# Batch 0's token softmax and reads in mid-run, with its x loaded a second time, and a new order of all steps

## The chip, the cores and the metric

One core of one Trainium2 chip. The metric is device time in microseconds (us) of one launch. The kernel before takes 210.89 us, the median of three runs (210.84 to 211.17).

## The reference

Eight batches, each of eight heads with 512 tokens and 32 states of 64 numbers, attend in both directions; the results go, 4352 rows of 512, through a two-layer network with a Prelu of its own slope for each of 2048 hidden columns.

```python
scores = scale * np.matmul(x, state.transpose(0, 1, 3, 2))
a = softmax(scores)                                  # over the 32 states
xread = np.matmul(a, state)                          # 512 rows a batch
scores2 = scale * np.matmul(state, x.transpose(0, 1, 3, 2))
a2 = softmax(scores2)                                # over the 512 tokens
sread = np.matmul(a2, x)                             # 32 rows a batch
rows = concatenate([xread, sread])                   # heads side by side
h = rows @ w_in
out = (maximum(h, 0) + alpha * minimum(h, 0)) @ w_out
```

## The kernel before, in words

Everything is one function. Every piece of work is a named step, and a table of tokens, `ORDER`, says in which order the steps are given to the engines: `F.1.9.4` is "first product of batch 1, hidden block 9, in PSUM bank k4", and the letter `a`, `v` or `p` at some tokens picks ScalarE (ACT), VectorE (DVE) or GpSimd (POOL). Each engine works its part of the list strictly in that order and waits where an operand is not there yet. DMAs that cast (x, states, w_in, w_out) are issued from POOL, transposing DMAs and the stores of the output from SyncE (SP).

For a batch b below 8 the rows of attention never exist as such. Steps `m` and `mo` form state times w_in for a quarter f of the hidden columns (`m_b_f`, L521, casts L545 and L547). The state softmax turns scores into weights: `sc` (L314), `sb` (a transpose in 32x32 blocks, L346), `smax` (L379), `ssh` (subtract the maximum, L384, on POOL), `sexp` (L393), `ssum` (L400, L401), `snorm` (L404), `wb` (transposed back, L412). Then `F` multiplies weights and m into h (L570), `N` takes the negative part of h on ACT (L623), and `G` makes the Prelu g on DVE (L626). Batch 0 is treated differently while the kernel starts: its state softmax runs in two halves on scores that have the tokens in the partitions (`tsc`, `at`), and four of its 16 hidden blocks are made by half parts `f`, `n`, `g` (L592, L607, L611).

The second layer is plain for batch 0 (`S`, L640, eight pairs for each of four blocks of 128 rows, and `O` for its output). For the other batches a scheme with seven in place of eight products is used: POOL or DVE form sums of g (`U`, L707) and of w_out (`W`, L683), `P` are the products (L728, four matmuls of 256 columns each), `K` and `Q` put the output together (L744, L759, L761).

The token softmax is the other direction: `tm` (maximum over 512 tokens, L424), `nb` (times -scale), `te` (exponential with its sum, L441), `tsum` (reciprocal), `tn` (each exponential times the reciprocal, L457 on ACT or L459 on POOL), `tt` (a transposing DMA), `rd` (times x, L475) and `rdo` (out of PSUM into `reads`, L486). After four batches `rt` and `rto` turn the reads into columns XS, and the 256 rows of all state reads make up a ninth batch: its `F` (L579) contract XS with w_in.

x is loaded by `lx` into one of three buffers xg (L161); `xd` transposes it by DMA. For batches 0 and 1 `xt` and `xo` do so by matmuls and copies (L299, L304), and batch 0's x comes without a cast through SP in two halves that `cx` casts (L177). The states of batch 0 come in a small early load through ACT, all others in one load `lst` through POOL. `Z` are fills: matmuls of a pattern that nobody reads.

Of the kernel before, what the change touches and what calls it, by code (L numbers as in the profile page):

```python
# [8 lines left out]
F32 = mybir.dt.float32  # L9
# [13 lines left out]
m.1.0 mo.1.0.v f.0.0.0.2 n.0.1.0 snorm.p.0.1 xt.1.0.0.0 at.1.1 ao.1.v n.0.0.0 xo.1.0.1.a g.0.1.0.0 g.0.0.0.1 m.0.1.3.1
xo.1.0.0.a sc.1 m.2.0.4.0 mo.0.1.a.1 mo.0.1.a.0 mo.2.0.a.0 g.0.0.0.0 S.0.2.0.1 mo.2.0.a.1 tm.1 sb.1 F.0.5.2 F.0.4.3
nb.1.a wo.1 g.0.1.0.1 wi.3 f.0.1.1.4 N.0.5 G.0.5 F.0.6.0 te.1.0 smax.1 N.0.4 S.0.2.1 G.0.4 F.0.7.5 te.1.1 f.0.0.1.2
m.0.2 N.0.6 n.0.1.1 G.0.6 g.0.1.1.1 mo.0.2.a g.0.1.1.0 wo.2 wo.3 tsum.0 S.0.1.2.3 S.0.2.2 F.0.11.0 N.0.7 G.0.7 ssh.p.1
n.0.0.1 F.0.10.4 g.0.0.1.0 g.0.0.1.1 S.0.1.1 N.0.11 G.0.11 sexp.1 ssum.1.5 m.0.3 mo.0.3.a S.0.2.3 S.0.1.3 S.0.1.0
m.1.1 N.0.10 G.0.10 tn.0.0.p mo.1.1.a tn.0.1.p tt.0 F.0.9.2 snorm.v.1 F.0.8.0 N.0.8 m.1.3 N.0.9 G.0.9 S.0.1.5 mo.1.3.a
W.1.0.p F.0.14.4 N.0.14 F.0.15.5 N.0.15 S.0.2.5 m.1.2 mo.1.2.a G.0.8 S.0.2.4 wb.1 lx.2 G.0.14 xd.2 F.0.13.2 N.0.13
S.0.1.4 F.1.5.0 N.1.5 F.0.12.4 G.0.15 S.0.1.7 W.2.0.p F.1.1.5 G.0.13 W.3.0.p S.0.2.7 N.0.12 G.0.12 tsum.1 F.1.6.2  # L30
W.3.1.p G.1.5 N.1.1 W.1.1.p G.1.1 N.1.6 G.1.6 S.0.1.6 F.1.4.4 F.1.12.0 O.0.1.a N.1.4 N.1.12 G.1.4 F.1.8.5 N.1.8 G.1.12
F.1.15.3 F.1.2.2 G.1.8 S.0.2.6 N.1.15 G.1.15 W.2.1.p S.0.0.3.4 N.1.2 S.0.0.1 rd.0.0 lx.3 tn.1.0.a sc.2 O.0.2.a G.1.2
m.2.2.5.3 mo.2.2.a.1 rdo.0.a sb.2 tn.1.1.p mo.2.2.a.0 F.1.3.1 tm.2 S.0.3.0.2 W.4.1.p F.1.0.3 N.1.0 smax.2 N.1.3 G.1.3
S.0.3.4 F.1.13.0 N.1.13 S.0.0.5 nb.2.a te.2.1 S.0.3.2 ssh.p.2 G.1.0 U.1.3.0.p F.1.7.5 N.1.7 te.2.0 G.1.7 tsum.2
S.0.3.6 S.0.3.5 S.0.3.7 F.1.14.1 N.1.14 G.1.13 S.0.3.3 G.1.14 tn.2.0.p tt.1 U.1.1.1.p U.1.2.1.p xd.3 sexp.2 S.0.0.2
m.2.3.3.5 m.4.3 mo.2.3.a.0 ssum.2.0 mo.2.3.a.1 S.0.0.0 F.1.9.1 N.1.9 mo.4.3.a G.1.9 S.0.3.1 S.0.0.6 O.0.3.a snorm.v.2
P.1.2.0.1.3 F.1.11.5 N.1.11 G.1.11 wb.2 m.3.2 mo.3.2.a S.0.0.7 F.1.10.1 N.1.10 G.1.10 S.0.0.4 O.0.0.a rd.1.2 rdo.1.a
m.3.0.0.5 mo.3.0.a.1 lx.4 xd.4 sc.3 tm.3 P.1.2.1.1 mo.3.0.a.0 sb.3 F.2.9.4 N.2.9 G.2.9 nb.3.a F.2.11.2 F.2.10.5
# [63 lines left out]
def kernel(  # L102
# [710 lines left out]
```

## Time and profile before

| | |
|---|---|
| median of three runs | 210.89 us |
| the profiled execution | 210.96 us, of which its span is 209.2 us |
| PE busy | 199.0 us (95%) |
| DVE busy | 182.0 us (87%) |
| POOL busy | 165.6 us (79%) |
| ACT busy | 150.9 us (72%) |
| read from HBM / written | 17.31 / 8.91 MB |

Times in the profile run from the start of the span. A group's row gives line, engine, operation, out<-in with shapes, count, then busy us and mean ns of one, then the idle time just before and what ended it. A matmul's own duration overlaps the next one's: what a matmul costs in a row of many is the step from start to start. The same holds in a smaller measure for DVE and ACT.

### The profile page before, as it was taken

Reading aid. Unit: us, or ns where it says so; the run is one execution under the profiler, and the core shown is the slowest. Engines: PE = TensorE matmul, PEld = TensorE weight load, DVE = VectorE, ACT = ScalarE, POOL = GpSimd, SP = SyncE. Lnnn points to the kernel's source line nnn. Section 1 sums busy time; section 2 is a strip of 40 time slices with the busy share of each in tenths; the row PEclk is TensorE's granted clock in tenths of the full one; section 3 lists DMA queues with packets and bytes.
Section 4 is the critical chain, followed back from the end, with each engine's and each line's share of the span. In section 5 each row is a group of like instructions: output and inputs, shape, how many; then the busy total and the mean of one; then the engine's idle time right before and its main releaser. Section 6 shows DMA issues by size and latency. Waiting matters only on the chain.

```text
span 209.2 us, 5108 instructions
## 1 busy us (share of the span) xinstructions
PE 199.0 (95%) x2024; PEld 132.9 (64%) x2024; DVE 182.0 (87%) x275; ACT 150.9 (72%) x293; POOL 165.6 (79%) x105
## 2 busy tenths in 40 slices
PE   7787799999999999999999999999999999999993
PEld 2453333443667677666577776667778777788882
DVE  0899999999999999999999999999899868595750
ACT  3799998999999889998897748956876386423000
POOL 8244599899999999998999999897981999504640
PEclk9999999999999999999999999999999999999999
DMA  6999999698586698269981572034201111013142
GB/s 167 219 204 206 206 188 130 154 156 161 120 104 147 125 93 194 68 90 168 141 109 39 104 165 97 12 93 127 75 3 53 50 50 53 0 50 103 60 150 95
DMA packets 49992, 23.71 MB, mean 113 GB/s; under 512 B 34480, under 2 KB 49456, under 8 KB 49968
## 3 DMA queue, kind: packets, MB, share of 16 engines
q0 software_dynamic: 17792, 8.09, 30.1%
q1 hardware_dynamic: 31904, 15.22, 29.6%
q8 instruction: 16, 0.26, 0.5%
q10 hardware_dynamic: 272, 0.07, 0.1%
q14 instruction: 8, 0.07, 0.1%
HBM read 17.31 MB, written 8.91 MB: 125 GB/s over the span
## 4 chain that ended last, share of the span: by engine, by line
PE 61%; DMA 12%; DVE 11%; POOL 11%; issue 1%; ACT 0%; SPq 0%; POOLq 0%; DVEq 0%
PE px L728 19%; PE h L570 16%; PE pv L728 9%; POOL gsum L707 7%; DVE g L626 6%; PE py L728 6%; DMA w_in_sb<-in_moe_w_in_dram 5%; DMA st<-in_state_dram 4%; PE h L579 3%; PE o L640 2%; PE m_ps L521 2%; DMA xT<-xg 2%; DMA e2T<-e 2%; DVE oq L761 1%; DVE nb L424 1%
## 5 line engine op out<-in xcount | busy, mean ns | idle before, releaser
L626 DVE SCALAR_TENSOR_TENSOR g<-neg,oma_sb,h 128x512 f16<-128x512 f32 (+1 forms) x140 | 92.3, 707 | 7.4 <-ACT neg L623 6.8
L623 ACT ACTIVATE neg<-h 128x512 f32<-128x512 f32 (+1 forms) x140 | 75.1, 579 | 20.6 <-PE h L570 15.5
L570 PE MATMUL h<-aT,m 128*128 128x512 f16 x248 | 67.3, 379 | 0.2
L728 PEld LDWEIGHTS <-gsum 128*128 128x128 f16 x480 | 46.2, 98 | 13.0 <-issue 1.5
L728 PEld LDWEIGHTS <-g 128*128 128x128 f16 x360 | 35.1, 98 | 11.2 <-issue 0.9
L707 POOL TENSOR_TENSOR gsum<-g,g 128x1024 f16<-128x1024 f16 (+1 forms) x14 | 27.8, 1990 | 11.6 <-DVE g L626 7.2
L707 POOL TENSOR_TENSOR gsum<-gsum,g 128x1024 f16<-128x1024 f16 (+1 forms) x15 | 30.0, 2003 | 8.3 <-DVE gsum L707 7.5
L570 PEld LDWEIGHTS <-m 128*128 128x128 f16 x248 | 23.8, 98 | 16.1 <-issue 1.9
L728 PE MATMUL px<-ws,gsum 128*128 128x256 f16 x240 | 32.8, 273 | 0.0
L707 POOL TENSOR_TENSOR gsum<-g 128x1024 f16<-128x1024 f16 (+1 forms) x14 | 28.8, 2064 | 0.8 <-PE pv L728 0.8
L707 POOL TENSOR_TENSOR gsum<-g,gsum 128x1024 f16<-128x1024 f16 x12 | 25.4, 2130 | 0.2
L744 ACT COPY kept<-px 128x512 f32<-128x512 f32 (+1 forms) x20 | 11.5, 577 | 11.3 <-PE px L728 9.5
L547 ACT CAST m<-m_ps 128x512 f16<-128x512 f32 x33 | 18.0, 604 | 1.9 <-PE m_ps L521 1.7
L640 PE MATMUL o<-w_out_sb,g 128*128 128x512 f16 x64 | 17.5, 380 | 1.8 <-DVE g L626 1.0
L384 POOL TENSOR_TENSOR ts<-ts,mx 128x1024 f32<-128x1024 f32 x7 | 13.4, 1913 | 5.9 <-DVE mx L379 5.9
L728 PE MATMUL py<-w_out_sb,g 128*128 128x256 f16 x120 | 17.5, 273 | 0.1
L728 PE MATMUL px<-w_out_sb,g 128*128 128x256 f16 x120 | 16.7, 272 | 0.1
L728 PE MATMUL px<-w_out_sb,gsum 128*128 128x256 f16 x120 | 16.7, 273 | 0.0
L728 PE MATMUL pv<-ws,gsum 128*128 128x256 f16 x120 | 16.1, 273 | 0.0
L728 PE MATMUL pv<-ws,g 128*128 128x256 f16 x120 | 15.7, 273 | 0.0
L761 DVE TENSOR_TENSOR oq<-pv,kept 128x512 f32<-128x512 f32 (+1 forms) x16 | 10.4, 652 | 5.2 <-PE pv L728 4.8
L521 PE MATMUL m_ps<-w_in_sb,stT 64*32 64x512 f16 x256 | 12.6, 384 | 1.1 <-DMA w_in_sb<-in_moe_w_in_dram 0.4
(84 smaller groups left out, 253.6 us busy)
## 6 DMA issues: line engine op xcount, KB each, us to landing
out_dram<-oq SPq DMA_DIRECT2D x28, 256.0 KB, 2.7
xg<-in_x_dram POOLq DMA_DIRECT2D x7, 512.0 KB, 7.1
w_in_sb<-in_moe_w_in_dram POOLq DMA_DIRECT2D x4, 512.0 KB, 11.3
w_out_sb<-in_moe_w_out_dram POOLq DMA_DIRECT2D x4, 512.0 KB, 13.4
x<-in_x_dram SPq DMA_DIRECT2D x2, 512.0 KB, 5.0
out_dram<-osb SPq DMA_DIRECT2D x4, 256.0 KB, 2.7
out_dram<-oq SPq DMA_DIRECT2D x4, 128.0 KB, 2.1
st<-in_state_dram POOLq DMA_DIRECT2D x1, 224.0 KB, 7.5
```

The source lines that it names most:

```text
L384: engine(e).tensor_tensor(blocks(cols(live["ts", b], j, S)), blocks(scored(b, j)), over_blocks(cols(live["mx", b], j, S // N)), ALU.subtract,)
L521: nc.tensor.matmul(t[N * k : N * (k + 1), :], st_head(b, h)[64 * r : 64 * r + 64, :], w_in_sb[64 * r : 64 * r + 64, c, 512 * f : 512 * (f ...
L547: copier(e)(m_tile(b, f)[:, g, :], t[g])
L570: nc.tensor.matmul(h.rearrange("p (r j s) -> p r j s", r=2, j=2), ms[b, f][:, g, 128 * j : 128 * (j + 1)], weights(b, g), start=(g == 0), ...
L579: nc.tensor.matmul(h, w_in_sb[:, c, 128 * jc : 128 * (jc + 1)], XS[:, c].rearrange("p q n b -> p (q n b)"), start=(c == 0), stop=(c == n_c ...
L623: nc.scalar.activation(neg, h, RELU, bias=0.0, scale=-1.0)
L626: nc.vector.scalar_tensor_tensor(g_tile(b, jc), negs.pop((b, jc)), oma_sb[:, jc : jc + 1], hs.pop((b, jc)), ALU.mult, ALU.add,)
L640: nc.tensor.matmul(outs[b, q], g_tile(b, jc)[:, 128 * q : 128 * (q + 1)], w_out_sb[:, jc, :], start=not begun and jc == 2 * jc2, stop=left ...
L707: engine(e).tensor_tensor(t, x(), y(), op)
L728: nc.tensor.matmul(pbanks[b, name][:, i, :], of(b, c)[:, j, 128 * i : 128 * (i + 1)], moving[:, 4 * c + j, :], start=not begun and j == 0, ...
L744: copier(e)(t, pbanks[b, "x"])
L761: nc.vector.tensor_tensor(osb, pbanks[b, name], kept[b, add], ALU.add)
```

## The change

Seven things at once; the largest is that `ORDER` is a new list throughout, 1111 tokens for 1115, with other PSUM banks and some other engines.

1. Batch 0's token softmax and reads leave the start. In the start its x has the name `first`; in mid-run x of batch 0 is loaded again (`lx.0`), transposed by DMA (`xd.0`), and scored as the other batches are (`sc.0` whole, in place of two halves).
2. `tn` is gone. The reads are scaled by the reciprocal on leaving PSUM, in two halves a batch.
3. The early state load brings batches 0 and 1; `lst` has the other six and comes after all of w_in.
4. The pattern of the fills is half as wide and read twice.
5. w_in pieces 1, 0, 2, x of batch 1, w_in 3, states, w_out 2, 0, 1, 3 is the new order of loads.
6. Casts of m: in the start, products with w_in of batches 1, 2, 3 and 5 come ahead of the first `F` of batch 1; before, batches 4, 1 and 2 had some of theirs there.
7. Other engines for some steps: three more `U` on DVE (late in the run), one half of batch 0's normalization on DVE in place of POOL, both casts of x's first half on DVE. The counts:

| step | before | after |
|---|---|---|
| tn on ACT / POOL | 6 / 10 | 0 / 0 |
| rdo on ACT / DVE | 8 / 0 | 15 / 1 |
| U on POOL / DVE | 55 / 9 | 52 / 12 |
| K on ACT / DVE | 20 / 4 | 22 / 2 |
| mo on ACT / DVE | 45 / 6 | 47 / 4 |
| nb on ACT / DVE | 4 / 4 | 7 / 1 |
| snorm on POOL / DVE | 2 / 7 | 1 / 8 |
| lx, xd, sc | 7, 6, 9 | 8, 7, 8 |

```diff
-            xgs[0] = att.tile([128, H, 2, 2, D], F16, name="xg_0", tag="xg", bufs=3)
+            xgs["first"] = att.tile([128, H, 2, 2, D], F16, name="xg_first", tag="xg", bufs=3)
...
-    n_j = (B * H * N - n0) // 128
-    st0_32 = consts.tile([128, 2, D], F32)
-    nc.scalar.dma_start(st0_32, rows[:n0, :].rearrange("(g p) d -> p g d", p=128))
+    n_j = (B * H * N - 2 * n0) // 128
+    st0_32 = consts.tile([128, 4, D], F32)
+    nc.scalar.dma_start(st0_32, rows[: 2 * n0, :].rearrange("(g p) d -> p g d", p=128))
...
-    pattern = consts.tile([128, 512], F16)
+    pattern = consts.tile([128, 256], F16)
...
+        twice = pattern.unsqueeze(1).to_broadcast([128, 2, 256])
         for _ in range(n):
-            nc.tensor.matmul(t, pattern[:, :128], pattern, start=True, stop=True)
+            nc.tensor.matmul(
+                t.rearrange("p (a n) -> p a n", a=2), pattern[:, :128], twice, start=True, stop=True
+            )
...
     def x_transposed(b, j, g, k):
+        b = b or "first"
...
-            live["r2", b] = att.tile([128, 2], F32, name=f"r2_{b}", tag="r2", bufs=2)
+            live["r2", b] = att.tile([128, 2], F32, name=f"r2_{b}", tag="r2", bufs=4)
...
-    def token_norm(b, g, e):
-        e2 = live["e2", b][:, g, :, :]
-        r2 = live["r2", b][:, g : g + 1]
-        if e == "a":
-            nc.scalar.mul(e2, e2, r2)
-        else:
-            nc.gpsimd.tensor_scalar(e2, e2, r2, 1.0, ALU.mult, ALU.mult)
...
-    def state_reads_out(b, e):
-        copier(e)(reads[:, b % 4], live.pop(("sr", b)))
+    def state_reads_out(b, g, e):
+        to, t, r2 = reads[:, b % 4, g, :], live["sr", b][:, g, :], live["r2", b][:, g : g + 1]
+        if e == "a":
+            nc.scalar.mul(to, t, r2)
+        else:
+            nc.vector.tensor_scalar_mul(to, t, r2)
```

One line of the table, the first, before and after:

```
Z.1.1 Z.2.1 stc.a cx.0.0.a stt.3 wi.0 sbd.0.a Z.4.1 cx.0.1.v xt.0.0.1.5 xo.0.0.1.a sbd.1.v xt.0.0.0.0 xo.0.0.0.v
Z.1.1 Z.2.1 Z.3.1 wi.1 cx.0.1.v stc.0.a stt.0.4 sbd.0.a xt.0.0.1.5 sbd.1.a cx.0.0.v xt.0.0.0.0 Z.1.1 xo.0.0.1.v
```

First place: POOL at the start of the program, from the first load on, before.

```order
L207 DMA w_in_sb<-in_moe_w_in_dram 128x4x512
L201 DMA st<-in_state_dram 128x896
L161 DMA xg_142<-in_x_dram 128x8x256
L207 DMA w_in_sb<-in_moe_w_in_dram 128x4x512
L213 DMA w_out_sb<-in_moe_w_out_dram 128x4x512
L207 DMA w_in_sb<-in_moe_w_in_dram 128x4x512
L404 TENSOR_TENSOR an_156<-ts_153,r_0_155 128x512 x2
L213 DMA w_out_sb<-in_moe_w_out_dram 128x4x512
L207 DMA w_in_sb<-in_moe_w_in_dram 128x4x512
L213 DMA w_out_sb<-in_moe_w_out_dram 128x4x512 x2
```

The same place after the change:

```order
L207 DMA w_in_sb<-in_moe_w_in_dram 128x4x512 x3
L411 TENSOR_TENSOR an_153<-ts_150,r_0_152 128x512
L161 DMA xg_193<-in_x_dram 128x8x256
L207 DMA w_in_sb<-in_moe_w_in_dram 128x4x512
L201 DMA st<-in_state_dram 128x768
L213 DMA w_out_sb<-in_moe_w_out_dram 128x4x512 x4
```

Three pieces of w_in now go first, the states stand behind all of w_in, and of the two normalizations one (the first half's) is left here.

Second place: ACT from the exponential of batch 1 (L393 before, L400 after) on, before; `neg_0_...` and `neg_1_...` are negative parts of batches 0 and 1, `m_1_1` is m of batch 1, quarter 1.

```order
L393 ACTIVATE ts_1_416<-ts_1_416 128x1024
L545 CAST m_0_3_520<-m_ps0_3_511 128x1024
L623 ACTIVATE neg_0_10_537<-h_0_10_496 128x512
L545 CAST m_1_1_541<-m_ps1_1_528 128x1024
L623 ACTIVATE neg_0_8_553<-h_0_8_550 128x512
L623 ACTIVATE neg_0_9_564<-h_0_9_546 128x512
L545 CAST m_1_3_569<-m_ps1_3_555 128x1024
L623 ACTIVATE neg_0_14_576<-h_0_14_573 128x512
L623 ACTIVATE neg_0_15_581<-h_0_15_578 128x512
L545 CAST m_1_2_594<-m_ps1_2_585 128x1024
L623 ACTIVATE neg_0_13_609<-h_0_13_606 128x512
L623 ACTIVATE neg_1_5_616<-h_1_5_613 128x512
```

The same place after:

```order
L400 ACTIVATE ts_1_444<-ts_1_444 128x1024
L548 CAST m_5_2_544<-m_ps5_2_515 128x1024
L550 CAST m_5_0_546<-m_ps5_0_0_505 128x512
L550 CAST m_5_0_546<-m_ps5_0_1_506 128x512
L626 ACTIVATE neg_0_13_551<-h_0_13_539 128x512
L548 CAST m_1_3_580<-m_ps1_3_553 128x1024
L550 CAST m_2_3_582<-m_ps2_3_0_562 128x512
L550 CAST m_2_3_582<-m_ps2_3_1_563 128x512
L550 CAST m_3_0_608<-m_ps3_0_0_597 128x512
L548 CAST m_1_2_612<-m_ps1_2_584 128x1024
L626 ACTIVATE neg_1_14_626<-h_1_14_623 128x512
L626 ACTIVATE neg_1_2_636<-h_1_2_633 128x512
```

Batch 0 has one negative part in these rows instead of six; casts of m, some of later batches, stand between.

Third place: POOL in mid-run, from the subtraction of batch 3's maximum (L391 after) to the first sum of batch 2, after the change. `xg_1252` is the second load of batch 0's x; `gsum_4_1` is sum 4, half 1, of a batch.

```order
L391 TENSOR_TENSOR ts_1001<-ts_1001,mx_1002 128x1024
L710 TENSOR_TENSOR gsum_4_1_1103<-g_3_631,gsum_2_1_1074 128x1024
L710 TENSOR_TENSOR gsum_4_0_1229<-g_2_655,gsum_2_0_1027 128x1024
L710 TENSOR_TENSOR gsum_3_0_1245<-g_0_638 128x1024
L161 DMA xg_1252<-in_x_dram 128x16x128
L710 TENSOR_TENSOR gsum_3_1_1314<-g_1_660 128x1024
L710 TENSOR_TENSOR gsum_1_0_1335<-g_0_1076,g_2_1015 128x1024
```

Before, from the same subtraction (L384) to the first sum of batch 2:

```order
L384 TENSOR_TENSOR ts_999<-ts_999,mx_1000 128x1024
L459 TENSOR_SCALAR e_3_1056<-e_3_1056,r_3_1057 128x512
L707 TENSOR_TENSOR gsum_4_1_1255<-g_3_673,gsum_2_1_839 128x1024
L707 TENSOR_TENSOR gsum_4_0_1264<-g_2_681,gsum_2_0_1112 128x1024
L683 TENSOR_TENSOR ws_781<-w_out_sb,ws_624 128x1024
L707 TENSOR_TENSOR gsum_1_0_1271<-g_0_1042,g_2_1009 128x1024
```

The normalizations (L459) are gone, and the load of x stands between two sums. Behind it, on SP, `xd.0` waits for it, and on PE `sc.0`.

More of the change, by code (lines that the diff above doesn't have):

```diff
@@ L23 @@
[L23 to L27, printed above, removed]
@@ L176, in x0_cast @@
     def x0_cast(j, g, e):
[L177 removed]
+        copier(e)(xgs["first"][:, 4 * g : 4 * g + 4, j, :, :], x0s[j][:, 4 * g : 4 * g + 4, :, :])
     load_x0(0)
@@ L303, in x_out @@
     def x_out(b, j, g, e):
+        b = b or "first"
         copier(e)(x_tile(b)[:, 4 * g : 4 * g + 4, j, :], live.pop(("xp", b, j, g)))
@@ L354, in token_scores @@
                 live["tsc", j][:, :, 4 * g + k4, :],
-                live["xT", 0][:, h, j, :],
+                live["xT", "first"][:, h, j, :],
                 st_pairs[:, h, :, :],
```

183 lines of the change are left out of this document (94 added, 89 removed).

## The prediction

> **What bounds the kernel now.** The page's forty slices come first: which engine is full, and when.
>
> ```profile
> PE   7787799999999999999999999999999999999993
> PEld 2453333443667677666577776667778777788882
> DVE  0899999999999999999999999999899868595750
> POOL 8244599899999999998999999897981999504640
> ```
>
> PE shows nines from the sixth slice (26 us) to the last. DVE is full from the second slice to about 140 us, POOL in most of that stretch. The same by stage:
>
> ```profile
> 0.00:30.00 30.00, 23.95 (x270) 11.71 (x270) 24.12 (x46) 24.34 (x45) 17.68 (x25) 1.00 1.15 201
> 30.00:140.00 110.00, 109.58 (x1148) 69.31 (x1141) 107.87 (x148) 94.15 (x182) 106.43 (x59) 1.00 0.70 119
> 140.00:205.00 65.00, 64.73 (x614) 51.65 (x612) 49.55 (x82) 32.39 (x68) 41.46 (x23) 1.00 0.21 64
> ```
>
> The columns are PE, PEld, DVE, ACT and POOL busy, then clock, DMA share and GB/s. From 30 us PE misses 0.4 of 110 us, then 0.3 of 65. Who PE's two halves wait for after 35 us is in the list of waits (first line PE, the others PEld):
>
> ```profile
> PE sr_ps L475 <- DMA e2T<-e: 0.2, 1, 0.2
> PEld L521 <- issue: 3.5, 11, 0.4
> PEld L475 <- DMA e2T<-e: 0.5, 2, 0.3
> PEld L728 <- POOL gsum L707: 0.5, 2, 0.3
> PEld L640 <- DVE g L626: 0.3, 1, 0.3
> ```
>
> "Issue" is the hand-over between packed small matmuls and large ones, which the change keeps. Another engine is waited for during 0.2+0.5+0.5+0.3 = 1.5 us in 170. So the time is the moment at which PE has gone through its start, plus a fixed stock of matmuls, plus at most 1.5 us of waits, plus the tail after the last matmul. The chain of waits gives the matmuls' prices:
>
> ```profile
> 30.82 0.86 PE h L570 x4
> ...
> 199.62 3.06 PE px L728 x28
> ```
>
> That is 0.215 us for 512 columns and 0.109 for 256. Of these the change adds none. The question is how many are done early.
>
> **The start, by difference.** In before, DVE reaches its first Prelu part at 16.98 and the transposed weights of batch 1 at 32.18:
>
> ```profile
> 14.23 1.27 DVE L547 CAST m<-m_ps 128x512 f16<-128x512 f32 x2
> ...
> 15.51 1.23 DVE L545 CAST m<-m_ps 128x1024 f16<-128x1024 f32 x1
> ...
> 16.98 1.25 DVE L611 SCALAR_TENSOR_TENSOR g<-neg,oma_sb,h 128x256 f16<-128x256 f32 x3
> ```
>
> ```profile
> L424 DVE TENSOR_REDUCE nb<-sc 128x2 f32<-128x1024 f32 x8 | 9.6, 1206 | 0.0
> L177 DVE CAST xg<-x 128x512 f16<-128x512 f32 x2 | 0.9, 426 | 3.9 <-DMA x<-in_x_dram 3.9
> ```
>
> Ahead of that part the change takes from DVE the token maximum of batch 0 (1.2), two half casts for batch 4 (1.27), the wide cast for batch 1 (1.23) and three small operations (0.8 in all): 4.5 us. It adds two half casts of batch 0's own m (1.27), a normalization on 512 columns (0.6) and one cast of x, one copy of xT and the copy of the states (0.43 each at most): 3.1 us. The first part would start at 16.98-4.5+3.1 = 15.6; ACT's casts and two negative parts end there too, so I take 15.75.
>
> Then up to the weights of batch 1:
>
> ```profile
> 32.18 1.24 DVE L412 STREAM_TRANSPOSE aT<-an 128x1024 f16<-128x1024 f16 x1
> 33.34 2.84 DVE L626 SCALAR_TENSOR_TENSOR g<-neg,oma_sb,h 128x512 f16<-128x512 f32 x4
> ...
> 36.18 5.34 DVE L626 SCALAR_TENSOR_TENSOR g<-neg,oma_sb,h 128x512 f16<-128x512 f32 x8
> ```
>
> A Prelu in a row costs 0.66 (5.25 for eight), a half part 0.42 (1.25 for three). Before `wb.1` the new order has eight parts (3.4), all twelve full Prelus of batch 0 (7.9), two xT copies (0.8) and the state softmax of batch 1, six passes of 1.2 us and a reciprocal, overlapping by 0.06 each (7.3): 19.4 us. With some 0.5 us of waits for ACT, `wb.1` ends at 15.75+19.4+0.5 = 35.7. Before: 33.4. So the new kernel has all of batch 0 behind it and enters batch 1 later. ACT is next, which now casts m of batches 1, 2, 3 and 5 here:
>
> ```profile
> 17.56 2.05 ACT L547 CAST m<-m_ps 128x512 f16<-128x512 f32 x4
> ...
> 26.05 1.05 ACT L393 ACTIVATE ts<-ts 128x1024 f32<-128x1024 f32 x1
> ...
> 30.71 1.02 ACT L545 CAST m<-m_ps 128x1024 f16<-128x1024 f32 x1
> ```
>
> From the exponential of batch 1 (begins about 29.95) to its first negative part ACT runs that (1.05), three wide casts (3.0), five half casts (2.6) and one negative part of batch 0 (0.55): 7.2 us, to 37.2. The first Prelu of batch 1 is then ready to start at 37.8, where DVE, through with `wb.1`, one cast and one output copy, has been free since 37.05.
>
> Loads do not set this. In the chain of waits two of the long loads end at 10.38 and 26.54:
>
> ```profile
> 2.84 7.54 DMA st<-in_state_dram
> ...
> 15.97 10.57 DMA w_in_sb<-in_moe_w_in_dram
> ```
>
> Six 1 MB loads land in these 16.2 us, 2.7 us each. In the new order the first w_in piece takes the first place (9.3 us); the others follow at 12.0, 14.7, 17.4 (x of batch 1), 20.1, 21.1 (states), 23.8, 26.5, 29.2, 31.9 (w_out). Their first users on PE come at about 12.2, 15.3, 19.1, 22.4, 22.7, 25.6, 27.8, 31.0 and 33.8: always later, by 0.2 us at the tightest (`m.0.0`), and each microsecond that a load slips beyond costs about that. The larger first state load lands some 0.1 us later, hidden by x; the halved pattern saves POOL about 0.3 us before x is there, worth nothing.
>
> **PE at 48 us.** What before has done by then (L570, L640, L521 in this order):
>
> ```profile
> 0.00:48.00 48.00, 13.46 (x50) 4.72 (x50) 1.00 1.13 180
> 0.00:48.00 48.00, 14.62 (x54) 4.85 (x54) 1.00 1.13 180
> 0.00:48.00 48.00, 5.37 (x104) 1.68 (x104) 1.00 1.13 180
> ```
>
> Placing the new order's PE steps behind the Prelus and casts above, PE has at 48.1 us done 26 full first products (52 matmuls), 25 pairs of the second (50) and 13 of m (104). It lacks two matmuls net (0.43), and has one group of scores still to do that before had done in halves (0.24): **0.7 us behind**.
>
> **Later.** DVE, by contrast, is ahead:
>
> ```profile
> 0.00:48.00 48.00, 41.67 (x71) 1.00 1.13 180
> ```
>
> The new list has it through about 43 us of its work by 48 us, and is about 1 us shorter in all. POOL loses most:
>
> ```profile
> L459 POOL TENSOR_SCALAR e<-e,r 128x512 f16<-128x512 f16 x10 | 6.9, 694 | 0.5 <-ACT neg L623 0.4
> L457 ACT ACTIVATE e<-e,r 128x512 f16<-128x512 f16 x6 | 4.4, 735 | 0.1
> L486 ACT CAST XS<-sr_ps 128x128 f16<-128x128 f32 x8 | 2.3, 282 | 0.9 <-PE sr_ps L475 0.8
> L161 POOL DMA_DIRECT2D xg<-in_x_dram x7 | 8.2, 1169 | 0.6 <-DVE g L626 0.6
> L707 POOL TENSOR_TENSOR gsum<-g,g 128x1024 f16<-128x1024 f16 (+1 forms) x14 | 27.8, 1990 | 11.6 <-DVE g L626 7.2
> ```
>
> Ten normalizations (6.9), three sums given to DVE late (6) and one softmax half (1.05) go; one load issue (1.2) comes: 12.8 us less in all. ACT loses 4.4; its sixteen half-size scaled reads, not in this trace, cost between 0 and 0.28 each. I take 0.25 (nearest row 0.282), 4 us in place of 2.3, hidden: ACT is idle 16 of 110 us. The second token maximum, exponentials and reads are the same work at another time. So PE's 1.5 us of waits can only shrink by what POOL and DVE caused; I take half, 0.75, between 0 and 1.5.
>
> **Sum.** The profiled execution took 210.96 (span 209.2 and 1.76 around it), 0.07 above the median of 210.89. 210.96+0.7-0.75 = **210.9**. The tail has the same last product, addition and store, and the fills dropped from it start after the last product. By my placing the start could be off by 0.6 either way and the waits by 0.75, so this case's own range is 209.6 to 212.3, astride no change. A measurement here tells about 0.2% (0.4 us) from none.
>
> **Rivals.**
> - *The freed engines pay.* All 1.5 us of waits go and the start is level with before: 210.96-1.5 = **209.5**, or 208.9 with the start 0.6 early as well. For it: `wb.1` ends late, yet DVE's lead of over 1 us stays. Against: PE's order is fixed, and half of its waits are for e2T transfers.
> - *The second x comes late* (slower). PE stands at the mid-run scores `sc.0` until load and transpose are through, with everything behind it.
>
> ```profile
> DMA to landing us min/median/max: 6.3/7.1/9.6
> ```
>
> ```profile
> xT<-xg SPq DMA_TRANSPOSE x6, 4.3
> ```
>
> ```profile
> L384 POOL TENSOR_TENSOR ts<-ts,mx 128x1024 f32<-128x1024 f32 x7 | 13.4, 1913 | 5.9 <-DVE mx L379 5.9
> ```
>
> The first row is of the loads of x (tile xg). POOL starts the subtraction of batch 2 at about 48.05. Before it issues `lx.0` it has two subtractions (1.9), seven sums (2.05 with the step to the next) and two loads (1.2): 20.6 us, to 68.6. Landing (7.1) and transpose (4.3) give 80.0. PE, from 48.15, has 34 product groups (0.436), 25 first products (0.432), 7 second pairs (0.433), nine of m (0.3) and two each of scores and reads (0.6 a pair): 32.5 us, to 80.6. The margin is 0.6 us, so it decides once landing and transpose together take over 12 us. At the slowest landing, 9.6, PE waits 1.9 us: **212.8**, and 213.1 with the tail of the transpose held up a little. For it: two more transfers where DMA is already 0.70 busy, and a margin smaller than the spread of the landings. Against: the usual landing leaves the margin open, and any other wait of PE before 80 us widens the margin. [...]
> - *ACT's early casts bind.* If the seven-microsecond run of casts starts a microsecond late, DVE and PE begin batch 1 that much later, with nothing left to fill but second products: about +1.3, **212.2**. Against: ACT is not full up to 30 us (24.34).
> - *The clock falls back.* The start holds a few fills at other places:
>
> ```profile
> 1.46 3.60 PE L232 MATMUL fill<-pattern 128*128 128x512 f16 x8 [1.46 <-POOL pattern L192]
> ```
>
> Eight fills in 3.5 us are 0.44 each, half speed against 0.215 later; a spell of that at 8 to 14 us would double some 1.5 us of matmuls, of which about 1 us delays DVE: 212. [...]
>
> **Chances.** Forecast 0.47 (0.15 of it faster, 0.16 the same, 0.16 slower), freed engines 0.25, late x 0.14, casts 0.10, clock 0.02; in 0.02 the moves cancel wholly. Faster: 0.15+0.25 = 0.40. Same: 0.16+0.02 = 0.18. Slower: 0.16+0.14+0.10+0.02 = 0.42. Range: 208.9 (rival one's low end) to 213.1 (late x).
>
> **What would show it.** Right: first Prelu part near 15.75, `wb.1` ending near 35.7, about 102 matmuls of L570's and L640's kind by 48 us, PE waits after that under 1.5 us, and the last matmul near 205. Wrong: a wait of PE for xT at `sc.0` near 80 us; a wait of DVE for ACT of over 1 us near 37; PE matmul steps of 0.43 after 6 us; or PE full before 30 us, which would mean that I placed the start too late.

## The result, and the profile after

The changed kernel takes 214.03 us (median of four runs, 213.25 to 214.16) where the kernel before took 210.98 beside it: a ratio of 1.0127, with a 95% interval of 1.0100 to 1.0153. Run again among the experiments it came out at 1.0096 (1.0075 to 1.0117). It is slower, by 2.0 to 3.0 us. Its profiled execution took 214.16 with a span of 212.2, against 209.2.

The forty slices of the changed kernel, the same four engines as before and the granted clock:

```profile
PE   7888989999999999999999999999999999999992
PEld 2534433443666675776667775577867767788882
DVE  0799999999999999999999979999998986876641
POOL 6076079968999999999999999639980699100640
PEclk9999999999999999999999999999999999999999
```

PE, DVE and ACT are as full as they were; POOL is busy for 152.1 us in place of 165.6. The same by stage (PE, PEld, DVE, ACT, POOL, clock, DMA share, GB/s):

```profile
0.00:30.00 30.00, 25.15 (x219) 12.09 (x220) 23.01 (x46) 21.93 (x41) 12.65 (x21) 1.00 1.09 186
30.00:140.00 110.00, 108.80 (x1240) 67.44 (x1239) 106.05 (x144) 94.52 (x195) 102.10 (x52) 1.00 0.84 135
140.00:205.00 65.00, 64.31 (x524) 50.99 (x523) 53.74 (x85) 31.99 (x64) 36.24 (x19) 1.00 0.15 52
```

PE now stands for 1.20 us between 30 and 140 us (before 0.42) and for 0.69 behind it (0.27). The list of waits of PE's two halves from 35 us on, for other engines:

```profile
PE px L731 <- DVE kept L747: 0.7, 1, 0.7
PE o L643 <- DMA w_out_sb<-in_moe_w_out_dram: 0.3, 1, 0.3
PE m_ps L524 <- ACT e L448: 0.2, 1, 0.2
PEld L497 <- ACT XS L487: 0.3, 1, 0.3
PEld L573 <- ACT m L550: 0.3, 1, 0.3
PEld L573 <- ACT m L548: 0.3, 1, 0.3
```

That is 1.2 us of PE and 0.9 of its weight loads, where before had 0.2 and 1.3. The rest has to be read from PE's progress. For the table below, every matmul that has still to start is priced at its own step (0.216 us for 512 columns, 0.109 for 256, a packed group whole: 0.40 for eight of `m`, 0.46 for reads, 0.31 for scores). It shows how far PE is behind the kernel before, in us, at a time counted from the first fill (which starts 0.22 us earlier than in before); a negative number is a lead, and steps of 0.2 are noise of the counting. The other rows are experiments that follow.

| | at 35 | 100 | 110 | 190 | start of the last matmul, from the start of the span, against before's |
|---|---|---|---|---|---|
| the changed kernel | 1.0 | 1.7 | 2.5 | 2.5 | +3.1 |
| with more fills | -0.3 | 0.6 | 1.2 | 1.2 | +1.8 |
| with three edits | -0.3 | 0.5 | 0.4 | 0.5 | +0.6 |
| before, shifts on ACT | -0.2 | -0.1 | -0.1 | -1.3 | -1.3 |

There are three losses, at three places: 1.0 us up to 35 us, 1.5 between 35 and 190 us with a step of 0.8 at 100 to 110, and 0.8 in the tail; less the 0.2 by which the first fill starts earlier, that is the 3.1 of the last column. Each has an experiment.

### The profile page after: what moved, and what is told of

Same layout as the page of the kernel before. It is cut to its first block, busy times and chain, and to the rows that moved or that the text cites. A ratio compares the mean times of both kernels' runs of the same rounds, so it can differ in the third digit from the quotient of the medians.

```text
span 212.2 us, 5048 instructions
## 1 busy us (share of the span) xinstructions
PE 201.7 (95%) x2008; PEld 133.4 (63%) x2008; DVE 183.7 (87%) x275; ACT 149.7 (71%) x301; POOL 152.1 (72%) x92
## 4 chain that ended last, share of the span: by engine, by line
PE 61%; DVE 14%; DMA 11%; ACT 7%; issue 4%; POOL 2%; DVEq 0%; ACTq 0%; POOLq 0%
PE px L731 20%; PE h L573 15%; PE pv L731 10%; DMA w_out_sb<-in_moe_w_out_dram 8%; DVE g L629 8%; PE py L731 5%; PE h L582 3%; DMA st<-in_state_dram 2%; PE m_ps L524 2%; ACT e L448 1%; ACT neg L626 1%; PE sr_ps L474 1%; DVE mx L386 1%; DVE nb L431 1%; ACT XS L487 1%
## 5 line engine op out<-in xcount | busy, mean ns | idle before, releaser
L626 ACT ACTIVATE neg<-h 128x512 f32<-128x512 f32 (+1 forms) x140 | 74.1, 583 | 11.5 <-PE h L573 7.9
L573 PE MATMUL h<-aT,m 128*128 128x512 f16 x248 | 63.7, 379 | 0.5 <-DVE aT L375 0.2
L731 PEld LDWEIGHTS <-gsum 128*128 128x128 f16 x480 | 46.5, 98 | 11.3 <-issue 2.2
L710 POOL TENSOR_TENSOR gsum<-g,g 128x1024 f16<-128x1024 f16 (+1 forms) x13 | 26.6, 2056 | 30.5 <-DVE gsum L710 17.0
L731 PEld LDWEIGHTS <-g 128*128 128x128 f16 x360 | 34.9, 98 | 6.8 <-issue 0.8
L747 ACT COPY kept<-px 128x512 f32<-128x512 f32 (+1 forms) x22 | 12.5, 569 | 28.4 <-PE px L731 21.0
L731 PE MATMUL px<-ws,gsum 128*128 128x256 f16 x240 | 30.8, 273 | 0.8 <-DVE kept L747 0.7
L710 POOL TENSOR_TENSOR gsum<-gsum,g 128x1024 f16<-128x1024 f16 (+1 forms) x14 | 27.7, 1987 | 0.6
L710 POOL TENSOR_TENSOR gsum<-g 128x1024 f16<-128x1024 f16 (+1 forms) x13 | 26.8, 2074 | 0.0
L710 POOL TENSOR_TENSOR gsum<-g,gsum 128x1024 f16<-128x1024 f16 (+1 forms) x12 | 24.5, 2050 | 2.5 <-PE px L731 2.3
L391 POOL TENSOR_TENSOR ts<-ts,mx 128x1024 f32<-128x1024 f32 x7 | 13.4, 1913 | 11.2 <-DVE mx L386 8.7
L731 PE MATMUL py<-w_out_sb,g 128*128 128x256 f16 x120 | 16.7, 273 | 0.0
L731 PE MATMUL px<-w_out_sb,g 128*128 128x256 f16 x120 | 16.2, 273 | 0.0
L731 PE MATMUL pv<-ws,gsum 128*128 128x256 f16 x120 | 15.7, 273 | 0.0
L731 PE MATMUL px<-w_out_sb,gsum 128*128 128x256 f16 x120 | 15.6, 272 | 0.0
L731 PE MATMUL pv<-ws,g 128*128 128x256 f16 x120 | 15.4, 273 | 0.0
L548 ACT CAST m<-m_ps 128x1024 f16<-128x1024 f32 x13 | 13.4, 1033 | 1.0 <-PE m_ps L524 0.9
```

Of the source, the lines that this page charges most:

```text
L391: engine(e).tensor_tensor(blocks(cols(live["ts", b], j, S)), blocks(scored(b, j)), over_blocks(cols(live["mx", b], j, S // N)), ALU.subtract,)
L548: copier(e)(m_tile(b, f), t)
L573: nc.tensor.matmul(h.rearrange("p (r j s) -> p r j s", r=2, j=2), ms[b, f][:, g, 128 * j : 128 * (j + 1)], weights(b, g), start=(g == 0), ...
L626: nc.scalar.activation(neg, h, RELU, bias=0.0, scale=-1.0)
L710: engine(e).tensor_tensor(t, x(), y(), op)
L731: nc.tensor.matmul(pbanks[b, name][:, i, :], of(b, c)[:, j, 128 * i : 128 * (i + 1)], moving[:, 4 * c + j, :], start=not begun and j == 0, ...
```

## Experiments

Ratios are to runs of the kernel before on the same chip, with their 95% interval. Differences under 0.4% between two experiments are within these intervals; there the traces decide, and it is said. "Theory A" and the like are names that the expectations give to an explanation.

### The start: a gap of PE and the clock

In the changed kernel PE and DVE start so (start, us, engine, line, operation, count, idle time before and its releaser):

```profile
1.24 4.02 PE L233 MATMUL fill<-pattern 128*128 128x512 f16 x9 [1.24 <-POOL pattern L192]
6.06 0.43 PE L247 MATMUL st_ps<-ident,st 128*64 128x128 f16 x4 [0.80 <-ACT st L253]
6.42 1.03 PE L305 MATMUL xT_psfirst<-ident,xg_first 128*128 128x128 f16 x8
```

```profile
5.94 0.76 DVE L177 CAST xg_first<-x 128x512 f16<-128x512 f32 x2 [4.76 <-DMA x<-in_x_dram]
...
16.71 1.65 DVE L614 SCALAR_TENSOR_TENSOR g<-neg,oma_sb,h 128x256 f16<-128x256 f32 x4
```

The states land later (cast by ACT from 5.71 on, before 4.48), and x too (first cast 5.94, before 5.11). These times vary: in six profiled executions with the 64 KB load of before the states' cast starts at 4.48 to 4.97 and x's at 5.11 to 5.85; in eleven with 128 KB it is 5.25 to 5.75 (once 4.41) and 5.50 to 5.96. So the states are later by some 0.9 us, and x by little that can be told from this spread. PE has no more fills and stands for 0.80 us, until that cast of the states. The eight transposes then take 1.03 us, and the clock is full at 10.45 us by the trace's record; in before it was at 5.97.

**more_fills**, `fill(0, 6)` becomes `fill(0, 8)`:

> The changed kernel with eight instead of six fills at the very start, so that PE has no gap between its last fill (5.26 us) and the first transposes (6.06). Theory A, its part on the clock: the granted clock is full at about 6 us instead of 10.4, the transposes and scores of batch 0 up to 10 us run at twice the speed, the first Prelu part starts some 0.4 us earlier, and the time falls by about 0.4 us (213.6). Rival within A (the landing of x alone decides, transposes wait for it anyway): clock full early, time within 0.2 us. Theory B: within 0.2 us.

Measured: 212.81 us, ratio 1.0072 (1.0049 to 1.0094). PE of this run:

```profile
1.24 4.38 PE L233 MATMUL fill<-pattern 128*128 128x512 f16 x11 [1.24 <-POOL pattern L192]
5.88 0.30 PE L247 MATMUL st_ps<-ident,st 128*64 128x128 f16 x4 [0.26 <-ACT st L253]
6.28 0.73 PE L305 MATMUL xT_psfirst<-ident,xg_first 128*128 128x128 f16 x8
```

The clock is full at 4.98 us, the eight transposes take 0.73, the first Prelu part starts at 15.85, and PE is 0.3 us ahead of before at 35 us (table). **after_again**, the changed kernel unaltered, tells how often the gap costs:

> The changed kernel itself once more, as the level for the runs beside it. [...] Theory B: they agree within 0.3%, as those of before, at 213.5 to 214.

Measured: 213.25 us, 1.0096. Its six executions fall into two groups: spans of 211.7, 211.7 and 211.8, and of 210.8, 210.9 and 211.0. The four of the first measurement (211.5 to 212.2) lie with the longer ones. With more fills all but one of eleven are at 210.7 to 211.2, near the lower group. In the five profiled executions with six fills and this start the clock was full 2.7, 2.8, 3.5, 9.2 and 9.3 us after the first fill, so either early or late. In the late ones PE had its gap (4.0 to 4.8 us after the first fill) before the clock was full; in the early ones the clock rose during the fills, ahead of gaps of 0.9 to 1.4 us, and stayed up. That the gap is what made the rise late is my reading; what sets the moment of the rise was not shown. By that reading the gap costs 0.8 us in three of these six executions. In the profile of more_fills the clock had risen before the gap's place. In two later kernels that have its fills, fills_and_tail and three_edits, the clock rose behind the gap's place, now filled: it was full 6.0 and 5.5 us after the first fill, over 3 us before the late ones. The first Prelu part follows the clock: 15.85 to 16.00 us where it rose within 3.8 us of the first fill, 16.10 and 16.25 in these two, 16.71 and 16.76 in the late ones.

Splitting the state load was to bring x back. **split_states**:

```diff
-    nc.scalar.dma_start(st0_32, rows[: 2 * n0, :].rearrange("(g p) d -> p g d", p=128))
+    first_rows = rows[: 2 * n0, :].rearrange("(b g p) d -> b p g d", p=128, b=2)
+    nc.scalar.dma_start(st0_32[:, :2, :], first_rows[0])
...
         nc.sync.dma_start(alpha_rows[32 * q : 32 * q + n_jc, :], alpha_quarters[q])
+    nc.sync.dma_start(st0_32[:, 2:, :], first_rows[1])
```

> The changed kernel with its 128 KB load of first states cut in two: batch 0's 64 KB on ACT's queue as in before, batch 1's 64 KB on SP's queue behind x. Theory A (the larger load delays x and the first transposes): the first cast of x starts at about 5.1 us instead of 5.94, PE has no gap of 0.8 us at 5.3, the granted clock is full at 6 to 7 us instead of 10.4, the first Prelu part starts 0.8 to 1.0 us earlier (15.8), and the time falls by 0.8 to 1.0 us, to about 213.1. Theory B (what is lost lies in the order later: packed groups and waits in the stretch where PE is full): x is earlier all the same, but the time stays within 0.3 us of 214.0.

Measured: 217.11 us, 1.0265 (1.0235 to 1.0295). **split_states_2** has the second load ahead of `alpha`:

> The changed kernel with its 128 KB load of first states cut in two: batch 0's half on ACT's queue as in before, batch 1's half on SP's queue right behind x and ahead of alpha. Theory A: batch 0's states land at about 4 us, x about 0.5 us earlier than in the change, no gap of PE at 5.3 us, clock full at about 6 us, batch 1's states land at about 7 us, in time for their use at 7.8; first Prelu part at 15.5 or before; time 0.5 to 1.0 us below the changed kernel's. Theory B: the same start, but time within 0.3 us. If batch 1's states land past 8 us, ACT stands at their cast as it did with them behind alpha, and the run tells nothing of A.

Measured: 216.56 us, 1.0244 (1.0222 to 1.0266). ACT and the clock of the first of them:

```profile
4.76 0.30 ACT L255 CAST st<-st 128x128 f16<-128x128 f32 x1 [2.22 <-DMA st<-in_state_dram]
5.66 0.75 ACT L269 COPY st_pairs<-st_ps 64x256 f16<-64x256 f16 x2 [0.60 <-PE st_ps L249]
10.72 0.30 ACT L255 CAST st<-st 128x128 f16<-128x128 f32 x1 [4.31 <-DMA st<-in_state_dram]
```

```profile
PEclk9959999999999999999999999999999999999999
```

ACT casts batch 1's states at 10.7 us, in the second run at 9.8: their 64 KB land 6.0 and 7.9 us after their issue, with the DMA engines busy for 90% and more from 2.8 and 3.5 us on; batch 0's, issued at 0.74, took 4.0 and 4.5. ACT stands at that cast for 4.3 us, PE for 3.3, and the clock drops to half for 6.8 us, the 5 in the row. Neither run says what the larger load costs in time. The first does bear out theory A as far as the clock: batch 0's states are cast at 4.76, PE has no gap behind its fills, and the clock is full 5.8 us after the first fill, against 9.2 and 9.3 in the late executions of the changed start. **before_larger_load** asks it the other way:

```diff
-    nc.scalar.dma_start(st0_32, rows[:n0, :].rearrange("(g p) d -> p g d", p=128))
+    nc.scalar.dma_start(st0_32, rows[: 2 * n0, :].rearrange("(g p) d -> p g d", p=128))
```

The pattern of the fills moves into the memory of the reads, to make room.

> The kernel before with one part of the change: its first state load takes 128 KB (batches 0 and 1) instead of 64, with batch 1's half unused; the pattern of the fills lies in the memory of the reads so that there is room. Theory A (the larger load delays x): x's first cast starts at 5.9 instead of 5.1 us and the states' cast at 5.7 instead of 4.4; the first Prelu part comes up to 0.8 us later and the time rises by 0.4 to 0.8 us. Rival (the start has slack for it, as the prediction said): x later, time within 0.2 us.

Measured: 211.39 us, 1.0025 (1.0000 to 1.0051). The states' cast starts at 5.25 in place of 4.48, x's first at 5.50 in place of 5.11 (within the spread of the 64 KB load), the first Prelu part at 17.10 in place of 16.98. The clock is full at 5.54. The load costs 0 to 0.5 us by the interval, less than theory A said; nine of the twelve executions have spans of 209.3 to 210.0, three of 211.1 to 211.3, so that much of the difference may lie in a few long ones, of which there is no trace.

### The tail

PE and DVE at the end of the changed kernel:

```profile
199.99 1.47 PE L731 MATMUL pv<-ws,g 128*128 128x256 f16 x12
202.15 0.60 PE L731 MATMUL px<-ws,gsum 128*128 128x256 f16 x4 [0.69 <-DVE kept L747]
```

```profile
200.36 1.40 DVE L710 TENSOR_TENSOR gsum<-g 128x512 f16<-128x512 f16 x1
201.69 0.41 DVE L747 COPY kept<-px 128x256 f32<-128x256 f32 x1
```

The copy that frees the bank (`K.8.1`) stands on DVE behind a sum that takes 1.40 us and elsewhere 0.42. POOL is in sums of its own until 201.48; that they held this one up was not tried. **tail_keep_act**, `K.8.1.v` becomes `K.8.1.a`:

> The changed kernel with the kept copy K.8.1 of the last group on ACT instead of DVE, where it stands behind a sum (U.8.3.0) that takes 1.40 us. Theory C (the tail's 0.69 us wait of PE is the copy's place on DVE): the wait of the product line for that copy goes, the last product starts 0.6 us earlier, and the time falls by 0.5 to 0.7 us, to about 213.4. Rival (the sum on DVE is needed by PE soon after, or ACT's copy comes no earlier): the wait moves to the sum, and the time stays within 0.2 us.

Measured: 212.12 us, 1.0043 (1.0020 to 1.0067). The row `px L731 <- DVE kept` is gone from PE's waits and nothing has come in its place; between 190 us and the last matmul PE loses nothing more. The time fell by more than the 0.5 to 0.7 expected, in a profile whose clock was early. **fills_and_tail** has both edits:

> The changed kernel with eight fills at the start and the kept copy K.8.1 on ACT: both single edits together. If they are separate terms (clock at the start, a wait in the tail), the time falls by the sum of the two, some 1.2 to 1.8 us below the changed kernel, to about 212.2 to 212.8; if the two save the same time, it equals the better of them.

Measured: 212.34 us, 1.0063 (1.0042 to 1.0084): within the range, and by the time not told apart from either edit alone. Its trace has both gains: no wait in the tail and, at 35 us, PE 0.2 us behind.

### The middle: a small operation held on DVE

In the changed kernel, where PE loses 0.8 us, DVE and POOL show:

```profile
100.60 1.09 DVE L440 TENSOR_SCALAR nb<-nb 128x2 f32<-128x2 f32 x1
101.61 3.37 DVE L629 SCALAR_TENSOR_TENSOR g<-neg,oma_sb,h 128x512 f16<-128x512 f32 x5
```

```profile
97.33 2.13 POOL L710 TENSOR_TENSOR gsum<-g,g 128x1024 f16<-128x1024 f16 x1
99.54 4.21 POOL L710 TENSOR_TENSOR gsum<-gsum,g 128x1024 f16<-128x1024 f16 x2
```

1.09 us for two numbers a partition: `nb.5` ends at 101.69, when the first of POOL's two sums has ended (99.54 + 2.13 = 101.67). The Prelus queued behind it free the banks that PE's next first products need. **shift_alone**, `nb.5.v` becomes `nb.5.a`:

> The changed kernel with one edit: batch 5's token shift on ACT instead of DVE, where it took 1.09 us for 128x2 numbers beside a sum on POOL. Theory D: it frees 0.9 us of DVE at 100 us and does most of what the three edits did: ratio to before 1.004 to 1.008 where the changed kernel has 1.010 to 1.013. Rival (the waits of PE there are taken back by a later wait, and only fills and tail count): ratio 1.009 or more.

Measured: 212.97 us, 1.0079 (1.0053 to 1.0105): in theory D's range, but the interval reaches the rival's. The trace decides: counted as in the table, PE is 0.6 us behind at 100 us and 0.7 at 110, so the step is gone. **three_edits** has it with the two others:

> The changed kernel with eight fills and K.8.1 on ACT, and a third edit: the scaling of batch 5's token shift (128x2 numbers, 1.09 us on DVE at 100.6 while POOL is in a sum) on ACT. Theory D (in the middle PE waits because DVE frees the banks of first products late, where the new order sets many first products in a row): DVE gets 0.9 us at 100 us, the first two of six waits between first products (102.0 and 102.7 after the first fill, 0.22 us each) go, time 0.3 to 0.5 us below the two-edit kernel's (212.34, ratio 1.0063). Rival (these waits are taken back at a later wait, since DVE stays behind anyway): within 0.2 us of the two-edit kernel.

Measured: 211.39 us, 1.0003 (0.9979 to 1.0028), about 1 us below the two-edit kernel, twice what was expected, and level with before; in the table the step at 100 to 110 us is gone. **four_edits** moves `sb.7` to right behind `tm.7`:

> The three-edit kernel with a fourth: the transpose of batch 7's scores (sb.7) on DVE ahead of its second exponential instead of behind it, so that DVE does not stand 1.08 us for ACT at 123 us. Theory D: the waits between first products at 126 to 132 us shrink by half, another 0.3 to 0.5 us less. Rival: ACT's exponential of batch 7 now waits for DVE, the negative parts behind it come later, and the time is the same within 0.2 us or longer.

Measured: 211.85 us, 1.0007 (0.9979 to 1.0034). Two of the four waits between first products at 126 to 132 us go (0.74 us in all become 0.37), but the time doesn't tell it.

The kernel before has such operations too. **before_shift_act**: `nb.4`, `nb.6` and `nb.7` from `v` to `a`:

> The kernel before with the token shifts of batches 4, 6 and 7 on ACT instead of DVE; one of them takes 1.36 us on DVE at 138.3, beside sums on POOL. Theory D (DVE's loss counts only where PE waits for banks, and PE waits for nothing there): within 0.2% of before. Rival (a stretched small operation costs by itself): 0.5 to 1.0 us less than before.

Measured: 210.24 us, 0.9953 (0.9938 to 0.9969), span 207.9: faster than both kernels. My theory D fell here. In before the longest shift and PE behind it are:

```profile
138.34 1.36 DVE L433 TENSOR_SCALAR nb<-nb 128x2 f32<-128x2 f32 x1
139.61 2.05 DVE L626 SCALAR_TENSOR_TENSOR g<-neg,oma_sb,h 128x512 f16<-128x512 f32 x3
```

```profile
139.66 0.60 PE L728 MATMUL px<-w_out_sb,gsum 128*128 128x256 f16 x4
140.40 0.59 PE L570 MATMUL h<-aT,m 128*128 128x512 f16 x2
141.06 0.60 PE L728 MATMUL px<-w_out_sb,g 128*128 128x256 f16 x4
141.72 0.59 PE L570 MATMUL h<-aT,m 128*128 128x512 f16 x2
```

Four matmuls of 256 columns take 0.44 from start to start, two of 512 take 0.43. Here the steps are 0.74, 0.66 and 0.66: three gaps, 0.76 us, that the list of waits does not carry. A fourth (0.29) follows the shift at 118.6. Together 1.05, and all four are gone in the edited kernel.

**before_shift_dve** goes the other way: `nb.2`, `nb.3` and `nb.5` from `a` to `v`:

> The kernel before with the token shifts of batches 2, 3 and 5 on DVE instead of ACT, the reverse of the last edit, so that six of the eight stand there. Theory F (a shift on DVE is held until the sum that POOL is in has ended): by POOL's sums in the run of before (ends at 45.07, 57.33 and 86.98, shifts due at about 44.3, 55.4 and 86.3) the three take about 0.7, 2.0 and 0.7 us, each ending within 0.1 us of a sum's end on POOL, and the time rises by 1 to 3 us. Rival (the instruction takes 0.16 to 0.2 us by itself, and the long ones were chance): 0.2 us each, time within 0.2% of before.

Measured: 217.29 us, 1.0279 (1.0235 to 1.0322), 5.9 us. More than the 1 to 3 expected. Seven of the eight shifts now stand on DVE. Their row (count, shortest, median and longest in ns, first and last start), then one of them, and POOL beside it:

```profile
L432 DVE TENSOR_SCALAR nb<-nb x7: 160/1350/2102, 13.2 to 144.6; 128x2 f32<-128x2 f32 x7
```

```profile
90.75 2.10 DVE L432 TENSOR_SCALAR nb<-nb 128x2 f32<-128x2 f32 x1
```

```profile
88.63 2.12 POOL L706 TENSOR_TENSOR gsum<-g 128x1024 f16<-128x1024 f16 x1
90.71 2.11 POOL L706 TENSOR_TENSOR gsum<-g,gsum 128x1024 f16<-128x1024 f16 x1
92.81 0.69 POOL L458 TENSOR_SCALAR e<-e,r 128x512 f16<-128x512 f16 x1
```

0.16 us with POOL idle (13.2), 2.10 when a sum has just begun. The six that met an operation of POOL all end 0.02 to 0.04 us after it does (47.06 after 47.03, 61.07 after 61.05, 75.96 after 75.93, 92.85 after 92.82, 125.23 after 125.19, 145.91 after 145.89). That is a hold, not a price of the instruction, and it costs the whole: the three added holds are 1.49, 1.80 and 2.10 (expected from before's sums 0.7, 2.0 and 0.7; the later ones had moved), 5.4 us. With that of batch 4, which grew from 0.20 to 1.28, and that of batch 6, which shrank from 0.47 to 0.17, it is 6.2 against 5.9 measured.

Not every small operation of DVE is held. The reciprocals of the token softmax are of the same size and type, in before:

```profile
L451 DVE RECIPROCAL r<-r 128x2 f32<-128x2 f32 x8 | 1.2, 156 | 0.0
```

In this run and in before eleven of their sixteen stand wholly inside an operation of POOL, and each takes 0.15 to 0.17 us.

### The path of batch 0, and the freed engines

**no_second_path** leaves out, of the changed kernel, `lx.0`, `xd.0`, `sc.0`, `tm.0`, `nb.0`, `te.0`, `tt.0`, `tsum.0`, `rd.0` and `rdo.0`, with zeros in place of these reads:

> The changed kernel without batch 0's token path: the second load of x, its transpose, the scores, maximum, exponentials, transpose back and reads of batch 0 are left out, and their place among the reads is filled with zeros. Theory B (the path in the full stretch costs PE its two packed groups with their hand-overs, 0.33 + 0.40 us, and waits behind them): the time falls by 1.2 us or more, to 212.8 or less, and PE's waits between 48 and 145 us fall by half. Theory A (the start and the tail lose the time): it falls by the two groups alone, 0.5 to 0.8 us, to about 213.3, and PE at 48 us stands where it stood.

Measured: 211.67 us, 1.0009 (0.9988 to 1.0030), span 209.5; more_fills, whose clock was early too, has 210.9. **three_edits_no_path** does it where the three losses are gone:

> The three-edit kernel without batch 0's token path (second load, transpose, scores, maximum, exponentials and reads of batch 0 left out, zeros in their place). Theory B (the path costs its two packed groups with hand-overs, 0.7 to 0.8 us, and waits): 0.7 to 1.4 us below the three-edit kernel, ratio to before 0.993 to 0.997. If the path's price was mostly the token shift's neighbourhood (sums on POOL and the shift at 100 us, which stay without the path), it falls by 0.7 at most. If the path is hidden, within 0.2 us.

Measured: 210.33 us, 0.9973 (0.9950 to 0.9996); 1.1 us of median below three_edits, 0.3% by the ratios, and its last matmul starts 1.1 us earlier. Of that the two packed groups (scores, reads) are 0.8. So the path costs what PE does for it and little else: the late x is no part of it. Load, transpose and scores of the changed kernel:

```profile
69.44 1.18 POOL L161 DMA_DIRECT2D xg<-in_x_dram  x1
```

```profile
75.88 1.88 SPq L296 DMA_TRANSPOSE xT<-xg  x1
```

```profile
80.70 1.89 PE L573 MATMUL h<-aT,m 128*128 128x512 f16 x8
82.52 0.41 PE L321 MATMUL sc<-xT,stT 64*32 64x256 f16 x16
```

The load is issued at 69.44 (forecast 68.6), the transpose begins 6.4 us later, and PE reaches the scores at 82.52 without a wait.

**before_no_path** leaves the same steps out of before (with scaled reads):

> The kernel before with scaled reads and without batch 0's token path (scores, maximum, exponentials, transpose and reads of batch 0 left out, zeros in their place among the reads). What the path cost where it stood: if it lay in the slack of the start, the time falls by its reads alone, 0.3 to 0.6 us below before; if DVE's 1.4 us and ACT's 1.4 us for it at the start set the pace there, by 1 to 2 us. In the changed kernel the path cost 1.4 us of span (210.9 with eight fills against 209.5 without the path, both with an early clock): the difference between the two is the price of the move.

Measured: 212.32 us, 1.0039 (1.0019 to 1.0060): slower with less to do. PE waits 1.1 us for another batch's xT at its scores, a wait that before does not have. The price of the move can't be read from it, and stays open.

**before_scaled** changes nothing of before but `tn` (gone, all batches) and `rdo` (scaled, two halves on ACT):

> The kernel before with one part of the change alone: no normalization of the exponentials, the reads scaled by the reciprocal on leaving PSUM, in two halves on ACT; order, loads and states as in before. What the freed engines are worth (rival one of the prediction): if PE's waits are theirs, 0.5 to 1.5 us less, 209.5 to 210.5; if PE is full whatever POOL and ACT do, within 0.3 us of before. Slower only if ACT's sixteen small scaled reads cost more than the four large halves of the softmax that it loses.

Measured: 214.09 us, 1.0153 (1.0125 to 1.0180). With `tn` gone, batch 0's `tt` waits for its exponentials alone and starts at 15.55 in place of 26.42, among the loads of the weights. SP, and the longer of PE's two waits for w_out (2.8 us in all; before has one, of 0.8):

```profile
15.55 1.34 SPq L453 DMA_TRANSPOSE e2T<-e  x1
```

```profile
25.87 1.02 PE L634 MATMUL o<-w_out_sb,g 128*128 128x512 f16 x4 [2.28 <-DMA w_out_sb<-in_moe_w_out_dram]
```

**before_scaled_1to7** keeps `tn` for batch 0:

> The kernel before with reads scaled on leaving PSUM for batches 1 to 7 alone; batch 0 is normalized by POOL as in before, so that its transfer of exponentials starts at 26.4 us as in before and not at 15.6 as in the run with all batches scaled. Theory E (that run was 3 us slower because this one transfer and what it displaced stood among the loads of the weights: w_out landed 2 us later and PE waited 2.3 us): the time is that of before within 0.3 us, or up to 0.7 less. Rival (the scaled reads themselves cost, by ACT's sixteen small instructions or by later transfers that start too early): it stays 1 us or more above before.

Measured: 212.14 us, 1.0030 (1.0010 to 1.0050). Four fifths of the loss are gone, which fits the early transfer; that this one transfer held the loads back was not tried by itself. The rest, 0.6 us by the ratio, stays, so freed engines paid nothing here: counted as in the table PE is 0.4 us behind at 35 us and 1.1 at the end. Why is open.

## Why the prediction was wrong

**The frame held.** From 30 us on PE is full, and the time is start, stock, waits and tail. What failed is three terms, all with one sign: the start (+0.7 forecast, +1.0 measured), the waits (-0.75 forecast, +1.5 measured between 35 and 190 us) and the tail (0 forecast, +0.8 measured).

**The start.** The forecast row by row, in the profiled execution: first Prelu part 15.75, measured 16.71 (15.76 to 16.25 in the eight traces with the unsplit load whose clock was full by 7.2 us); `wb.1` ending at 35.7, measured 36.0; first Prelu of batch 1 at 37.8, measured 38.02. DVE's row of the end of the start:

```profile
34.76 1.24 DVE L419 STREAM_TRANSPOSE aT<-an 128x1024 f16<-128x1024 f16 x1
...
38.02 6.67 DVE L629 SCALAR_TENSOR_TENSOR g<-neg,oma_sb,h 128x512 f16<-128x512 f32 x10 [0.37 <-ACT neg L626]
```

About 102 large matmuls were forecast by 48 us; there are 52 + 49 = 101:

```profile
0.00:48.00 48.00, 13.65 (x52) 4.76 (x52) 1.00 1.13 176
0.00:48.00 48.00, 12.89 (x49) 4.48 (x50) 1.00 1.13 176
```

So counting Prelus and casts was right. Its term (0.7) measured 1.0 at 35 us and 1.4 at 48, in an execution with a late clock; in the six of these eight traces that keep batch 0's path it measured 0.1 to 0.8 at 48. The failed step is "Loads do not set this": "the larger first state load lands some 0.1 us later, hidden by x". It landed 1.3 us later (5.0 for 3.7 us from its issue; some 0.9 against the other traces), PE stood 0.80 us for it, and the clock was full at 10.45 us in place of 5.97. The 2 in 100 for the clock was my estimate, which no run shows; the runs showed a gap of 0.80 us with a clock that had yet to rise, and the rise 9.2 and 9.3 us after the first fill, where the gap was filled 5.5 and 6.0. "Matmul steps of 0.43 after 6 us" was named as a sign against the forecast and came; but as a clock that rose 4.5 us later than in before, while I looked only for one that falls back.

**The waits.** The failed step is "PE's 1.5 us of waits can only shrink". The rows of POOL and DVE said that their *sums* of work fell, and I took waits for a share of that. (DVE's did not even fall: it is busy for 183.7 us, before 182.0.) By the lists that the forecast used, the waits are 2.1 us, 0.7 of it in the tail. But between 35 and 190 us PE fell behind by 1.5, in gaps and hand-overs that no list shows. 0.7 to 0.8 were lost behind `nb.5`, held on DVE ahead of Prelus that PE needed; its edit shows that. The other 0.7 to 0.8 is open. The four waits between first products (0.75 in the changed kernel) are a candidate: the new order sets first products in longer rows (PE goes from a product of the second layer to a first product 45 times from 35 to 145 us in before, 18 times after). No run undid the order, though, and from one large matmul to the next the three-edit kernel loses no more than before, which has 1.05 us of such gaps of its own. The hand-overs to and from packed groups, which the forecast took as kept, are the other candidate: the "issue" rows of PE's weight loads add up to 13.8 us from 35 us on, in before to 10.3. The token shift stood in before's trace for all to read, 1.36 us for 128x2 numbers, and I passed over it because the list of waits had nothing behind it. Beside the 1.5 us of waits that I took for all there was to gain, 1.05 us lay in gaps that the list does not show.

**The tail.** "The tail has the same last product, addition and store" was the failed step: the same operations, but `K.8.1` on DVE behind a sum of 1.40 us, for which PE stood 0.69.

**The rivals.** The freed engines did not pay (before_scaled_1to7). The late x did not come: no wait at `sc.0`, for the landing was a usual one (6.4 us, in before 7.1 by the median). ACT's casts bound for 0.37 us, not more. ACT's scaled reads took 0.33 us each (forecast 0.25, at most 0.28). None of them was the loss; the range ended 0.9 us below the median.

**What the change is worth** without its three accidents: 1.0003, against 0.9953 for before without its held shifts. The best kernel here is the kernel before with three token shifts on ACT.

## What to carry to other kernels

Before forecasting a new order, look in the old trace for operations that take several times what their size says, and for what POOL does at that moment: here a TENSOR_SCALAR of 128x2 numbers on DVE cost up to the length of the sum that POOL was in (2.10 us of 2.11, 0.16 with POOL idle), and a reciprocal of the same size did not (0.15 to 0.17), so for such an operation the engine can matter more than the work. Read PE's steps from start to start, and not the list of waits alone: gaps of 0.2 to 0.3 us after a late bank added up to 1.05 us in before, beside 1.5 us of waits listed. And a load that was made larger, or issued where DMA was full, landed late itself (128 KB after 5.0 us for 64 KB after 3.7; 64 KB after 6.0 and 7.9 us with DMA busy for 90% and more), which showed as waits on engines that do no loading (PE 0.80 and 3.3 us), and beside the first of them as a clock full at 10.45 us in place of 5.97.

## What was not expected of the hardware

- A 128x2 operation on DVE took 0.16 us with POOL idle, and 0.47, 1.09, 1.36 and 2.10 beside POOL's sums of 2.13, ending each time within 0.04 us of the sum's end. Reciprocals of 128x2 took 0.15 to 0.17 inside POOL's operations.
- With a gap of PE of 0.8 us before the clock had risen it was full 9.2 and 9.3 us after the first fill, with that gap filled after 6.0 and 5.5; with gaps of 0.9 to 1.4 us just after it had risen, 2.7 to 3.5 us after the first fill, it stayed full.
- With one transposing DMA of 256 KB issued at 15.6 us in place of 26.4, PE waited 2.8 us for w_out in place of 0.8; that the one caused the other was not tried by itself.
